# One down-projection step ahead of the third unit's state products, the fourth unit's C scaled ahead of the last w_out issue, and the fourth unit's score and state products inside the third block

## The chip, the cores and the metric

The kernel runs on one core of a Trainium2 chip. The metric is the device time of one launch in microseconds (us); a time of a version is the median of several runs.

## The reference

Two layers follow each other. The first is a chunked state-space scan over 4 batches, 8 heads and 768 positions, with 32 values and 16 state entries a head; `L` is made from the running sums of `log a`. The second is a feed-forward layer with a squared ReLU on 3072 rows of 256 values, 2048 wide inside.

```python
CB = np.einsum('bhin,bhjn->bhij', Cc, Bc)
M = CB * L                                    # L: causal decay inside a chunk
y_intra = np.einsum('bhij,bhjd->bhid', M, xc)
y_inter = np.einsum('bhin,bhnd->bhid', Cc, state) * decay_to_i[:, :, :, None]
...
state = decay_full[:, :, None, None] * state + np.sum(Bx, axis=2)
...
x = attn_out.transpose(0, 2, 1, 3).reshape(B * S, H * D)
h = np.maximum(x @ w_in, 0.0)
return (h * h) @ w_out
```

## The kernel before

The work is cut into 12 **units**, numbered from 0: one batch and 256 of its 768 positions. A unit passes through these steps, whose two-letter tokens are used in the text.

- Loads of C, B and x (`ldC`, `ldB`, `ldx`, or `ld` for all three) are issued on SyncE's queue (SP). The eight weight pieces (`wi0` to `wi3` of w_in, `wo0` to `wo3` of w_out) are issued by GpSimd (POOL). `wo3` fills the tile `w_out_b3`, which the down-projection steps 6 and 7 of every block read.
- `pc` scales C and `pb` copies B, both into the tile `jt`; `px` scales x into `xs`. `pc` and `px` stand on POOL around the change; `pb3` stands on ScalarE (ACT).
- `tr` turns `jt` over: by transposes on TensorE (PE) for units 0 to 3, by a DMA on SP from unit 4 on. `tc` copies the result from PSUM to `bct`, on VectorE (DVE) for units 2 and 3.
- `mt` makes the scores in PSUM banks 0 to 3. They leave the banks by a mask on DVE (`mk`, line 252), or by a copy on ACT (`sc`, line 257) and a later mask from that copy (`ms`, line 261).
- `u` makes the unit's state products in columns 256 to 320 of two banks (line 268, out of `xs` and `jt`), `sf` turns the first of them into a scaled state `Sd` on DVE (line 396), `in` adds the masked scores times `xs`, `ca` adds the carried state. `t` copies the sum to the tile `T`, and `us` copies the state products to the tile `us` on ACT (line 349, or line 352 where the two banks aren't neighbours).

A unit's `T` then goes through the feed-forward layer as a **block** (block a is unit 0, b is unit 1, c is unit 2), in eight steps of 256 of the 2048 columns. `c5` is four matmuls with w_in into one bank (`c5@4` names bank 4) and a ReLU on ACT that writes `hb` and frees the bank; `qc5` squares `hb` into `h` on DVE; `C5` is four matmuls with w_out that add into the block's bank 6 or 7. There are four `hb` buffers. All of these matmuls have line 459, the ReLU line 482, the square line 488.

The order of all work is written out by hand, in the string `ORDER`. Each engine takes its own instructions in that order, so an instruction that waits holds up what stands behind it on its engine. A bank may be written again only when all that reads it is done: `c1@0` must wait until bank 0 has been read out. From unit 4 on one token, `rgN`, does the bulk of a unit.

Of the kernel before, what the change touches and what calls it, by code (L numbers as in the profile page):

```python
# [30 lines left out]
def kernel(  # L31
# [20 lines left out]
        pb1:a id2:512 tr1 id3:512 tc1:1:a tc1:0:v to wo0 ms0:p sf0 sk1 px1:p jz2:p wi2 mt1 ina0 inb0 ca0 pp1:a mk1 mk1 t0:aa  # L52
        us0 sc1 mk1 fr p2@4 u1:57:6 pd us1 a0@0 a1@1 ldC2:s ina1 ms1:v wo1 wi3 pc2 inb1 sf1 ca1 qa0 t1:vv a2@2
        ldB2:s qa1 a3@3 wo2 b0@4 qa2 qa3 qb0 b1@0 qb1 b2@1 b3@5 A0 A1 B0 pb2:p tr2@23 B1 zb0 qb3 gB3:v ldx2:s ldB3:s ldC3:s ldx3:s b4@0 a4@1
        iv:32:64 zb1 tc2:1:v tc2:0:v b5@4 sb1 sb0 qb4 a5@5 qb2 qa4 mt2 sc2 B3 iv:16:32 px2 wo3 pc3 px3 mk2 mk2 sc2 A3
        A2 ms2:v ms2:v qa5 a6@4 b6@5 pb3:a B2 a7@2 qb5 b7@3 u2:45 ina2 inb2 sf2 ld4 A4 tr3@01 ca2 tc3:1:v t2:aa B4 us2 B5
        tc3:0:v qa6 u3:45 pc4 mt3 A5 us3 sc3 c5@4 qb7 qb6 mk3 za3 pb4 ldC5:s ldB5:s c3@5 qa7 c4@0 qc5 c0@1 qc3 px4 tr4 ldx5:s pb5
        pc5 sa3 c1@4 c6@5 ldC6:s tr5 ldB6:s ldx6:s qc4 qc0 A6 px5 pq A7 wm c2@0 B6 c7@1 C0 ms3:v mk3 qc6 mk3 qc7 afC2 pc6 B7
        C3 C6 C4 qc1 bk rg4 C1 qc2 d1 d0 za4 sa4 pb6 mk4 mk4 d3 mk4 C5 d4 qd0 d2 mk4 px6 tr6 ld7 C2 C7 qd1 qd2 qd3 zb3
        rg5 sb3 D0 mk5 za5 sa5 D1 mk5 d5 qd4 D2 pc7 pb7 d6 qd5 d7 qd6 D3 zb2 e0 qd7 mk5 e1 qe0 sb2 D4 mk5 D5 tr7 ld8  # L60
        e2 qe1 D6 e3 qe2 ml px7 rg6 e4 D7 qe3 za6 sa6 zb6 mk6 e5 qe4 sb6 e6 qe5 e7 qe6 iv:64:96 mk6 E0 E1 E2 E3 ldC9:s
# [836 lines left out]
```

## Time and profile before

| | |
|---|---|
| median of 3 runs | 113.89 us (113.69 to 114.79) |
| the profiled execution | 114.1 us, of which the span from first to last instruction is 112.4 us |
| busy share of the span | PE 95%, weight loads 82%, DVE 75%, ACT 68%, POOL 44% |
| granted TensorE clock | 1.00 |
| moved by DMA | 13.44 MB, mean 120 GB/s |

Rows of the trace show the start in us from the first instruction, the duration in us, the engine, the line and the operation with output and input; `x16` is a count of merged instructions, and the last bracket gives the engine's idle time ahead of them and what ended it. PEld is the weight-load half of PE, SPq and POOLq are the queues that issue DMAs. Matmuls are pipelined, so that the durations of neighbours overlap: the distance from one start to the next is what a matmul costs.

### The profile page before, as it was taken

Reading aid. Unit: us, or ns where it says so; the run is one execution under the profiler, and the core shown is the slowest. Engines: PE = TensorE matmul, PEld = TensorE weight load, DVE = VectorE, ACT = ScalarE, POOL = GpSimd, SP = SyncE. Lnnn points to the kernel's source line nnn. Section 1 sums busy time; section 2 is a strip of 40 time slices with the busy share of each in tenths; the row PEclk is TensorE's granted clock in tenths of the full one; section 3 lists DMA queues with packets and bytes.
Section 4 is the critical chain, followed back from the end, with each engine's and each line's share of the span. In section 5 each row is a group of like instructions: output and inputs, shape, how many; then the busy total and the mean of one; then the engine's idle time right before and its main releaser. Section 6 shows DMA issues by size and latency. Waiting matters only on the chain.

```text
span 112.4 us, 3682 instructions
## 1 busy us (share of the span) xinstructions
PE 107.0 (95%) x1452; PEld 91.8 (82%) x1452; DVE 84.0 (75%) x191; ACT 76.1 (68%) x156; POOL 49.9 (44%) x97
## 2 busy tenths in 40 slices
PE   6898999989999999999999999999999999999990
PEld 2335799867998989989989989889899899899980
DVE  1679997927996899969997989779489298355440
ACT  1735893884894775685687686777876867867840
POOL 7589855068286737089038644364370020000000
PEclk9999999999999999999999999999999999999999
DMA  1999999969889699999993995899582030020203
GB/s 37 199 185 140 194 193 201 183 125 168 157 151 159 72 226 135 98 186 94 99 179 39 132 235 54 100 203 95 77 205 75 0 102 0 29 70 0 93 0 93
DMA packets 67281, 13.44 MB, mean 120 GB/s; under 512 B 63104, under 2 KB 65984, under 8 KB 67264
## 3 DMA queue, kind: packets, MB, share of 16 engines
q1 hardware_dynamic: 64320, 10.88, 60.3%
q0 software_dynamic: 1664, 2.10, 11.8%
q10 hardware_dynamic: 1280, 0.23, 1.1%
q8 instruction: 11, 0.18, 0.7%
q14 instruction: 6, 0.05, 0.1%
HBM read 10.58 MB, written 3.15 MB: 122 GB/s over the span
## 4 chain that ended last, share of the span: by engine, by line
PE 74%; DMA 15%; SPq 2%; POOL 2%; DVE 1%; issue 1%; ACT 0%; DVEq 0%; ACTq 0%; POOLq 0%
PE pp L459 66%; DMA x_nat<-in_x_dram 15%; PE pp L268 5%; PE pp L237 2%; SPq L138 1%; DVE mts L252 1%; PE pp L243 1%; POOL xs L195 1%; SPq L664 1%; POOL jt L175 1%; SPq L121 0%; PE pp L213 0%; DVE xs L195 0%; ACT osl L856 0%; DVEq L626 0%
## 5 line engine op out<-in xcount | busy, mean ns | idle before, releaser
L482 ACT ACTIVATE hb<-pp 128x512 bf16<-128x512 f32 x96 | 54.4, 600 | 22.2 <-PE pp L459 21.0
L459 PE MATMUL pp<-w_out_b,h 128*128 128x256 bf16 (+1 forms) x400 | 54.0, 268 | 0.0
L459 PE MATMUL pp<-T,w_in_b 128*128 128x256 bf16 x384 | 53.4, 273 | 0.0
L488 DVE TENSOR_TENSOR h<-hb 128x512 bf16<-128x512 bf16 x96 | 45.4, 492 | 10.7 <-ACT hb L482 10.0
L459 PEld LDWEIGHTS <-w_in_b 128*128 128x128 bf16 x384 | 41.5, 114 | 1.9 <-issue 1.1
L459 PEld LDWEIGHTS <-h 128*128 128x128 bf16 x400 | 37.6, 98 | 4.5 <-issue 1.0
L252 DVE TENSOR_TENSOR mts<-pp,mask 128x512 bf16<-128x512 f32 x43 | 28.5, 678 | 0.4 <-PE pp L237 0.2
L195 POOL TENSOR_TENSOR xs<-x_nat,Pinv 128x256 bf16<-128x256 f32 (+1 forms) x19 | 13.5, 729 | 16.4 <-DMA x_nat<-in_x_dram 8.6
L384 POOL TENSOR_TENSOR Sd<-z,Pquad 128x256 bf16<-128x256 f32 x16 | 11.0, 698 | 7.8 <-DVE z L368 6.0
L175 POOL TENSOR_TENSOR jt<-C_nat,P_sb 128x128 bf16<-128x128 f32 x22 | 10.0, 476 | 9.2 <-DMA C_nat<-in_C_dram 9.2
L368 DVE SCALAR_TENSOR_TENSOR z<-z,Ptot,us 128x64 f32<-128x64 f32 x8 | 3.1, 384 | 7.0 <-ACT us L352 5.1
L562 PE MATMUL pp<-const-bfloat16-1.0 128*128 128x512 bf16 (+2 forms) x18 | 6.2, 464 | 0.8 <-PEq L882 0.8
L510 ACT COPY osb<-pp 128x512 f32<-128x512 f32 x11 | 6.4, 583 | 0.4 <-PE pp L459 0.4
L183 POOL CAST jt<-B_nat 128x256 bf16<-128x256 f32 x9 | 3.7, 412 | 5.5 <-DMA B_nat<-in_B_dram 3.9
L268 PE MATMUL pp<-mts,xs 64*32 64x128 bf16 (+1 forms) x288 | 5.3, 219 | 0.0
L268 PE MATMUL pp<-bct,Sd 128*128 128x128 bf16 x40 | 4.2, 220 | 0.0
L268 PEld LDWEIGHTS <-xs 64*32 64x32 bf16 (+1 forms) x288 | 3.4, 93 | 0.6 <-issue 0.4
L268 PEld LDWEIGHTS <-jt 64*32 64x32 bf16 (+1 forms) x128 | 1.7, 90 | 2.4 <-issue 1.1
L562 PEld LDWEIGHTS <-const-bfloat16-1.0 128*128 128x128 bf16 x18 | 1.6, 112 | 2.4 <-issue 2.2
L268 PE MATMUL pp<-xs,jt 64*32 64x64 bf16 (+1 forms) x128 | 2.9, 196 | 0.6 <-POOL xs L195 0.5
L213 PEld LDWEIGHTS <-jt 128*128 128x128 bf16 x24 | 1.5, 97 | 2.3 <-ACT jt L183 1.0
L257 ACT CAST sc<-pp 128x512 bf16<-128x512 f32 x5 | 2.9, 609 | 0.7 <-PE pp L243 0.7
(78 smaller groups left out, 59.7 us busy)
## 6 DMA issues: line engine op xcount, KB each, us to landing
out_dram<-osb SPq DMA_DIRECT2D x11, 256.0 KB, 3.0
x_nat<-in_x_dram SPq DMA_DIRECT2D x6, 256.0 KB, 5.1
w_in_b<-in_moe_w_in_dram POOLq DMA_DIRECT2D x4, 256.0 KB, 6.1
w_out_b<-in_moe_w_out_dram POOLq DMA_DIRECT2D x4, 256.0 KB, 6.3
B_nat<-in_B_dram SPq DMA_DIRECT2D x6, 128.0 KB, 5.5
C_nat<-in_C_dram SPq DMA_DIRECT2D x12, 64.0 KB, 3.8
B_nat<-in_B_dram SPq DMA_DIRECT2D x12, 64.0 KB, 3.5
x_nat<-in_x_dram SPq DMA_DIRECT2D x6, 128.0 KB, 3.4
```

Of the source, the lines that this page charges most:

```text
L175: eng.tensor_tensor(out=_fap(jt[k % 3], 128 + 144 * g, [[384, 2], [32, 4], [1, 16]]), in0=_fap(loaded[k]["C"], 128 * g, [[16, 2], [32, 4], ...
L183: fn(out=_fap(jt[k % 3], 0, [[384, 2], [16, 2], [32, 4], [1, 16]]), in_=_fap(loaded[k]["B"], 0, [[16, 2], [128, 2], [32, 4], [1, 16]]))
L195: eng.tensor_tensor(out=_fap(xs, 256 * r, [[256, 2 // n], [32, 8], [1, 32]]), in0=_fap(loaded[k]["x"], 32 * r, [[32, 2 // n], [64, 8], [1, ...
L252: nc.vector.tensor_tensor(out=live[k]["mts"][:, q].rearrange("p r g i -> p (r g i)"), in0=pp[:, q, :], in1=mask1 if k >= LATE else mask, o ...
L268: nc.tensor.matmul(dst, w, v, start=bool(need), stop=False, skip_group_check=True, **({} if pos is None else {"tile_position": pos}))
L368: nc.vector.scalar_tensor_tensor(out=z, in0=prev[0], scalar=Ptot[:, total(1, b, j - 1):total(1, b, j - 1) + 1], in1=us, op0=ALU.mult, op1= ...
L384: nc.gpsimd.tensor_tensor(out=_fap(S_d, 0, [[128, 2], [32, 4], [1, 32]]), in0=_fap(z, 0, [[32, 2], [0, 4], [1, 32]]), in1=_fap(Pquad, 4 * ...
L459: nc.tensor.matmul(dst, w(0, 128), v, skip_group_check=True, **flags)
L482: nc.scalar.activation(out=hb.rearrange("p i t -> p (i t)"), in_=pp[:, h, :], func=AF.Relu)
L488: nc.vector.tensor_tensor(out=h2, in0=hb, in1=hb, op=ALU.mult)
L510: nc.scalar.copy(out=osb, in_=pp[:, 6 if blk == 1 else 7, :])
L562: nc.tensor.matmul(pp[:, h, 0:int(cols)], ones_b[:, 0:128], ones_b[:, 0:int(cols)] if dep is None else dep, start=True, stop=True, skip_gr ...
```

## The change

Four lines of `ORDER` change; no function does.

```diff
-        ... mt2 sc2 B3 iv:16:32 px2 wo3 pc3 px3 mk2 mk2 sc2 A3
-        A2 ms2:v ms2:v qa5 a6@4 b6@5 pb3:a B2 a7@2 qb5 b7@3 u2:45 ina2 inb2 sf2 ld4 A4 tr3@01 ca2 tc3:1:v t2:aa B4 us2 B5
-        tc3:0:v qa6 u3:45 pc4 mt3 A5 us3 sc3 c5@4 qb7 qb6 mk3 za3 pb4 ldC5:s ldB5:s c3@5 qa7 c4@0 qc5 c0@1 qc3 px4 tr4 ldx5:s pb5
-        pc5 sa3 c1@4 c6@5 ldC6:s tr5 ldB6:s ldx6:s qc4 qc0 A6 px5 pq A7 wm c2@0 B6 c7@1 C0 ms3:v mk3 qc6 mk3 qc7 afC2 pc6 B7
+        ... mt2 sc2 B3 iv:16:32 px2 pc3 wo3 px3 mk2 mk2 sc2 A3
+        A2 ms2:v ms2:v qa5 a6@4 b6@5 B2 a7@2 qb5 b7@3 pb3:a qa6 A4 u2:45:2 sf2 ina2 inb2 ld4 B4 ca2 t2:va B5 tr3@01 us2
+        A5 tc3:1:v tc3:0:v c5@4 qb6 pc4 c3@5 qb7 mt3 sc3 qa7 mk3 pb4 ldC5:s ldB5:s c4@4 qc5 c0@5 qc3 u3:01 us3 za3 px4 tr4 ldx5:s pb5
+        pc5 sa3 c1@0 c6@1 ldC6:s tr5 ldB6:s ldx6:s qc4 qc0 A6 px5 pq A7 wm c2@4 B6 c7@5 C0 ms3:v mk3 qc6 mk3 qc7 afC2 pc6 B7
```

A4, the fifth down-projection step of block a, goes ahead of the state products of unit 2 (`u2`), whose first half is written to bank 2 of its own (`u2:45:2`) and scaled (`sf2`) ahead of `in` on DVE. One half of T2 is copied by DVE instead of ACT, and `us2` becomes two copies. The transposes of unit 3 (`tr3`) move behind `ca2` and B5. The scores of unit 3 (`mt3`) move behind c5 and c3, and its state products (`u3`) behind c0, in banks 0 and 1 instead of 4 and 5; the block-c steps trade banks to match. On ACT the B copy of unit 3 (`pb3`) moves behind two ReLUs.

On **POOL**, in the stretch from the x of unit 2 (`xs2`) to the x of unit 3 (`xs3`), `jt0` is the target of `pc3` and `w_out_b3` that of `wo3`. Before:

```order
L195 TENSOR_TENSOR xs2_567<-x_nat2_497,Pinv_106 128x512 [waits DMAHW6_49,DVE_49]
L160 DMA w_out_b3_119<-in_moe_w_out_dram 128x1024
L175 TENSOR_TENSOR jt0_109<-C_nat3_500,P_sb_105 128x2x4x16 [waits DMAHW0_49,PE_49]
L175 TENSOR_TENSOR jt0_109<-C_nat3_500,P_sb_105 128x2x4x16 [waits PE_49]
L195 TENSOR_TENSOR xs3_572<-x_nat3_502,Pinv_106 128x512 [waits DMAHW1_49,PE_49]
```

Now:

```order
L195 TENSOR_TENSOR xs2_567<-x_nat2_497,Pinv_106 128x512 [waits DMAHW6_49,DVE_49]
L175 TENSOR_TENSOR jt0_109<-C_nat3_500,P_sb_105 128x2x4x16 [waits DMAHW0_49,PE_49]
L175 TENSOR_TENSOR jt0_109<-C_nat3_500,P_sb_105 128x2x4x16 [waits PE_49]
L160 DMA w_out_b3_119<-in_moe_w_out_dram 128x1024
L195 TENSOR_TENSOR xs3_572<-x_nat3_502,Pinv_106 128x512 [waits DMAHW1_49,PE_49]
```

The issue of the last w_out piece stands behind the two scalings of C, which wait for a DMA. The queue of SP keeps its order.

On **ACT**, from the last ReLU of block a and b to the ReLU of c1 (`hb2_1` is the output of c1's ReLU, `sc3_0` the score copy of unit 3). Before:

```order
L183 CAST jt0_109<-B_nat3_495 128x2x2x4x16
L482 ACTIVATE hb0_7_611<-pp_120 128x512
L482 ACTIVATE hb1_7_619<-pp_120 128x512
L226 CAST T2_691<-pp_120 128x4x64 x2
L349 COPY us2_698<-pp_120 128x128
L349 COPY us3_746<-pp_120 128x128
L257 CAST sc3_0_748<-pp_120 128x512
L482 ACTIVATE hb2_5_754<-pp_120 128x512
L482 ACTIVATE hb2_3_770<-pp_120 128x512
L482 ACTIVATE hb2_4_778<-pp_120 128x512
L482 ACTIVATE hb2_0_786<-pp_120 128x512
L482 ACTIVATE hb2_1_806<-pp_120 128x512
```

Now:

```order
L482 ACTIVATE hb0_7_610<-pp_120 128x512
L482 ACTIVATE hb1_7_618<-pp_120 128x512
L183 CAST jt0_109<-B_nat3_495 128x2x2x4x16
L226 CAST T2_689<-pp_120 128x4x64
L352 COPY us2_703<-pp_120 128x64 x2
L482 ACTIVATE hb2_5_716<-pp_120 128x512
L482 ACTIVATE hb2_3_726<-pp_120 128x512
L257 CAST sc3_0_747<-pp_120 128x512
L482 ACTIVATE hb2_4_761<-pp_120 128x512
L482 ACTIVATE hb2_0_769<-pp_120 128x512
L349 COPY us3_789<-pp_120 128x128
L482 ACTIVATE hb2_1_807<-pp_120 128x512
```

The copy of unit 3's state products (`us3`) stood ahead of all of block c's ReLUs and now stands behind four of them and the score copy.

On **PE**, from c0 (the first of its matmuls) past `u3` to A6, in the changed kernel, with the waits; `T2` is block c's input and `h20_6` is A6's:

```order
L459 MATMUL pp_120<-T2_689,w_in_b0_112 128x256 [waits Activation_49]
...
L268 LDWEIGHTS jt0_109 [waits Activation_49]
L268 MATMUL pp_120<-xs3_572,jt0_109 32x64 [waits Pool_49]
...
L268 MATMUL pp_120<-xs3_572,jt0_109 32x64 [waits DVE_49]
...
L459 MATMUL pp_120<-T2_689,w_in_b0_112 128x256 [waits Activation_49]
...
L459 MATMUL pp_120<-w_out_b3_119,h20_6_621 128x256 [waits DMASW7_49]
```

Behind c0 stand the three waits of `u3` (on the score copy that clears bank 0, on `xs3`, and on the direct mask that clears bank 1), then that of c1 on `us3`, which reads bank 0, and that of A6 on the landing of `w_out_b3`. Before, `u3` stood ahead of all of block c and c1 used bank 4.

More of the change, by code (lines that the diff above doesn't have):

```diff
@@ L54 @@
         ldB2:s qa1 a3@3 wo2 b0@4 qa2 qa3 qb0 b1@0 qb1 b2@1 b3@5 A0 A1 B0 pb2:p tr2@23 B1 zb0 qb3 gB3:v ldx2:s ldB3:s ldC3:s ldx3:s b4@0 a4@1
-        iv:32:64 zb1 tc2:1:v tc2:0:v b5@4 sb1 sb0 qb4 a5@5 qb2 qa4 mt2 sc2 B3 iv:16:32 px2 wo3 pc3 px3 mk2 mk2 sc2 A3
-        A2 ms2:v ms2:v qa5 a6@4 b6@5 pb3:a B2 a7@2 qb5 b7@3 u2:45 ina2 inb2 sf2 ld4 A4 tr3@01 ca2 tc3:1:v t2:aa B4 us2 B5
-        tc3:0:v qa6 u3:45 pc4 mt3 A5 us3 sc3 c5@4 qb7 qb6 mk3 za3 pb4 ldC5:s ldB5:s c3@5 qa7 c4@0 qc5 c0@1 qc3 px4 tr4 ldx5:s pb5
-        pc5 sa3 c1@4 c6@5 ldC6:s tr5 ldB6:s ldx6:s qc4 qc0 A6 px5 pq A7 wm c2@0 B6 c7@1 C0 ms3:v mk3 qc6 mk3 qc7 afC2 pc6 B7
+        iv:32:64 zb1 tc2:1:v tc2:0:v b5@4 sb1 sb0 qb4 a5@5 qb2 qa4 mt2 sc2 B3 iv:16:32 px2 pc3 wo3 px3 mk2 mk2 sc2 A3
+        A2 ms2:v ms2:v qa5 a6@4 b6@5 B2 a7@2 qb5 b7@3 pb3:a qa6 A4 u2:45:2 sf2 ina2 inb2 ld4 B4 ca2 t2:va B5 tr3@01 us2
+        A5 tc3:1:v tc3:0:v c5@4 qb6 pc4 c3@5 qb7 mt3 sc3 qa7 mk3 pb4 ldC5:s ldB5:s c4@4 qc5 c0@5 qc3 u3:01 us3 za3 px4 tr4 ldx5:s pb5
+        pc5 sa3 c1@0 c6@1 ldC6:s tr5 ldB6:s ldx6:s qc4 qc0 A6 px5 pq A7 wm c2@4 B6 c7@5 C0 ms3:v mk3 qc6 mk3 qc7 afC2 pc6 B7
         C3 C6 C4 qc1 bk rg4 C1 qc2 d1 d0 za4 sa4 pb6 mk4 mk4 d3 mk4 C5 d4 qd0 d2 mk4 px6 tr6 ld7 C2 C7 qd1 qd2 qd3 zb3
```

## The prediction

> **What bounds the kernel now.** I first read TensorE's busy time by stretch, then its rows, then the rows of whatever released it. By stretch (core 0's busy time, granted clock, DMA share, GB/s):
>
> ```profile
> core 0: us, PE busy (x), PEclk, DMA share, GB/s
> 24.00:24.60 0.60, 0.09 (x17) 1.00 0.73 166
> 24.60:27.30 2.70, 2.65 (x78) 1.00 1.14 183
> 28.00:31.00 3.00, 3.00 (x30) 1.00 0.83 156
> 31.00:35.00 4.00, 4.00 (x39) 1.00 0.99 172
> 35.00:109.40 74.40, 74.40 (x982) 1.00 0.65 100
> ```
>
> From 28.0 to 109.4 us TensorE has no gap, at full clock. So whatever its work at 31 us gains or loses reaches the end, whole: nothing behind it has slack to give back. All that can be won here lies in the hole at 24.0 to 24.6 and in small stops up to 27.3. These are TensorE's rows there, and two of its weight loads:
>
> ```profile
> 22.98 1.04 PE L459 MATMUL pp<-T,w_in_b 128*128 128x256 bf16 x8
> 24.53 0.26 PE L268 MATMUL pp<-xs,jt 64*32 64x64 bf16 x16 [0.51 <-POOL xs L195]
> 25.10 0.61 PE L459 MATMUL pp<-w_out_b,h 128*128 128x256 bf16 x4
> 25.55 0.72 PE L213 MATMUL pp<-eye_b,jt 128*128 128x128 bf16 x6
> 25.86 0.23 PEld L213 LDWEIGHTS <-jt 128*128 128x128 bf16 x4 [0.22 <-POOL jt L175]
> 26.10 0.28 PE L268 MATMUL pp<-bct,Sd 128*128 128x128 bf16 x2
> 26.21 1.04 PE L459 MATMUL pp<-w_out_b,h 128*128 128x256 bf16 x8
> 27.18 0.21 PEld L268 LDWEIGHTS <-jt 64*32 64x32 bf16 x13 [0.21 <-ACT us L349]
> 27.26 0.26 PE L268 MATMUL pp<-xs,jt 64*32 64x64 bf16 x16
> 27.44 0.42 PE L243 MATMUL pp<-bct 32*64 32x256 bf16 x16
> 27.80 0.61 PE L459 MATMUL pp<-w_out_b,h 128*128 128x256 bf16 x4
> 28.24 2.78 PE L459 MATMUL pp<-T,w_in_b 128*128 128x256 bf16 x24
> 30.86 1.04 PE L459 MATMUL pp<-w_out_b,h 128*128 128x256 bf16 x8
> ```
>
> In order: a7 and b7, `u2` (waits for `xs2`), A4, `tr3` (waits for `pc3`), `ca2`, B4 and B5, `u3` (waits for `us2`), `mt3`, A5, the six steps c5, c3, c4, c0, c1, c6, and A6 with A7. A step of four matmuls costs (30.86 - 28.24) / 6 = 0.44 us.
>
> **The gain, worked out.** Three stops go. The step ahead of `u2` fills the hole: `u2` starts at 24.53 in both, since the x of unit 2 decides it, and A4 (0.44 us) is done before it, at 24.3 by slots. The stop at `tr3` (0.22, from `pc3`) goes, since `pc3` is earlier and `tr3` later. The stop at `u3` (0.17 of start to start, 27.09 to 27.26) goes from there. Together 0.83 us. The transposes, `u3` and `mt3` keep their counts.
>
> Its slots after, by the same row distances: `u2` 24.53, B4 25.10, `ca2` 25.55, B5 25.66, `tr3` 26.10 (six at 0.06, as four took from 25.86 to 26.10), A5 26.43, c5 26.87, c3 27.31, `mt3` 27.74, c4 28.10. If nothing else waited, A6 would start at 30.86 - 0.83 = 30.03. Two things are late next.
>
> **First, the scalar engine's order.** These rows are of ACT and of DVE:
>
> ```profile
> 27.61 0.27 ACT L349 COPY us<-pp 128x128 f32<-128x128 f32 x1 [0.66 <-PE pp L268]
> 27.91 0.59 ACT L257 CAST sc<-pp 128x512 bf16<-128x512 f32 x1
> 28.93 3.05 ACT L482 ACTIVATE hb<-pp 128x512 bf16<-128x512 f32 x6 [0.43 <-PE pp L459]
> 26.30 0.62 DVE L228 COPY bct<-pp 128x384 bf16<-128x384 bf16 x2 [0.63 <-PE pp L213]
> 26.84 1.73 DVE L488 TENSOR_TENSOR h<-hb 128x512 bf16<-128x512 bf16 x3
> 28.49 0.68 DVE L252 TENSOR_TENSOR mts<-pp,mask 128x512 bf16<-128x512 f32 x1
> ```
>
> A ReLU starts 28.93 - 28.24 = 0.69 after its step; the six follow each other every 0.48 and the last takes 0.64. Before, `us3` and `sc3` ran while TensorE was at A5, and the ReLUs had 0.43 idle ahead of them. After, in ACT's order: c5's ReLU 27.56, c3's 28.04, `sc3` 28.52 to 29.11, c4's ReLU 29.0, c0's 29.48, `us3` 29.96 to 30.23. With 0.05 from a release to TensorE (24.48 to 24.53 at `xs2`), c4 starts at 28.2, c0 at 28.69, and `u3` at 29.16. Its second half also needs the mask of bank 1. DVE copies `bct3` 0.2 after `tr3`, from 26.63; three squares and the mask follow as above, 0.33 later than before: the mask ends at 28.49 + 0.33 + 0.68 = 29.50, `u3`'s second half starts at 29.55, and 27.61 - 27.26 = 0.35 later `us3` could start. So ACT's queue (29.96) decides by a hair, with DVE at 29.90 close behind.
>
> c1 goes to bank 0, which `us3` reads: it starts at 30.28, c6 at 30.72, **A6 at 31.16**, which is 0.30 later than the 30.86 of before. TensorE stands still for some 0.6 us between `u3` and c1, where it never stood before. If POOL's C scalings slow the squares less in their new place, only the 29.90 moves, not the 29.96.
>
> **Second, the last w_out piece.** POOL's rows, SP's issue of the third C, and landing times of DMAs:
>
> ```profile
> 23.43 1.05 POOL L195 TENSOR_TENSOR xs<-x_nat,Pinv 128x512 bf16<-128x512 f32 x1 [3.98 <-DMA x_nat<-in_x_dram]
> 24.42 0.61 POOL L160 DMA_DIRECT2D w_out_b<-in_moe_w_out_dram  x1
> 25.05 0.77 POOL L175 TENSOR_TENSOR jt<-C_nat,P_sb 128x128 bf16<-128x128 f32 x2
> 26.15 1.05 POOL L195 TENSOR_TENSOR xs<-x_nat,Pinv 128x512 bf16<-128x512 f32 x1 [0.34 <-DMA x_nat<-in_x_dram]
> 18.07 1.90 SPq L138 DMA_DIRECT2D C_nat<-in_C_dram  x1
> C_nat<-in_C_dram SPq DMA_DIRECT2D x1, 128.0 KB, 6.4
> w_out_b<-in_moe_w_out_dram POOLq DMA_DIRECT2D x1, 256.0 KB, 5.9
> DMA to landing us min/median/max: 5.9/6.3/7.1
> DMA to landing us min/median/max: 5.6/6.1/8.3
> ```
>
> (The last two rows are of all four w_out and all four w_in pieces; the row above them is that of `wo3`.) Before, the piece landed at 24.42 + 5.9 = 30.3, and A6 wanted it at 30.86: 0.5 us to spare. After, `pc3` comes first, and C of unit 3 lands only at 18.07 + 6.4 = 24.5; with 0.1 to start and 0.77 of work POOL issues `wo3` at 25.3. Landing is a new unknown. From below, a load of the same 256 KB on SP a little later took 3.6 us:
>
> ```profile
> x_nat<-in_x_dram SPq DMA_DIRECT2D x1, 256.0 KB, 3.6
> ```
>
> That would be 28.9 and free. From above, 8.3 gives 33.6, 2.8 us late. I take its own 5.9: the DMA share in its flight is no lower after the shift (1.14, 0.83, 0.99 above). So it lands at 31.2, and **A6 starts at 31.26**.
>
> The Trainium skill ("DMA: Bandwidth & Descriptors", section "Anatomy of one DMA — SWDGE (gpsimd) path") fits such a load as 2.0 us plus bytes over 436 KB per us, an estimate of 2.6 us here. By that the piece would be there long before A6, and the sum would rest on `us3` alone, +0.3. This trace disagrees, with 5.6 at the least in eight loads among other traffic.
>
> **The sum.** The two waits lie over each other, so the later counts: 31.26 - 30.86 = +0.4. The 0.83 won is spent by 31 us, and 0.4 more. The other edits cost nothing:
>
> ```profile
> L228 DVE CAST T<-pp 128x256 bf16<-128x256 f32 x2 | 0.7, 416 | 0.0
> L352 ACT COPY us<-pp 128x64 f32<-128x64 f32 x6 | 1.3, 243 | 0.0
> ```
>
> The `T2` half on DVE (0.42 us) and the two `us2` copies (0.24 each) fall beside B5, `tr3` and A5 with c5 not due until 26.87; if that cover went, each would cost at most its own length. `pb3` behind two ReLUs ends near 25.1, a microsecond ahead of `tr3`; SP's issues keep their order; `px3` waits for its x until 26.15 either way, as the issue of `wo3` ends at 25.9. Behind A6, qc0 and bank 4 and 5 are ready a microsecond before C0 and c2 want them.
>
> Against the profiled execution that is 114.1 + 0.4 = 114.5; the median of before lies 0.2 lower, so I forecast 113.89 + 0.4 = **114.3 us** for the median.
>
> **The rivals.**
>
> *The gain is kept.* If the piece lands in time and ACT and DVE are quick enough that c4, c0 and `u3` keep their slots, `u3` starts at 28.98; `us3` still follows it by 0.35 and takes 0.27, so c1 starts at 29.65 and A6 at 30.53, which is -0.33: 113.6. The full 0.83 can't stay, since c1 needs `u3`'s own copy. For it speaks that the hole at 24.0 is surely filled. Against it, ACT must do four ReLUs and a score copy between 27.56 and `us3`, five at 0.48, which is 2.4 us. Chance 0.10.
>
> *No net change*, from 0.2 below to 0.2 above: ACT or DMA a little quicker than summed, gain and waits even. 0.16.
>
> *Slower, by late weights.* It is the landing of `w_out_b3` alone, at A6. It decides from a landing after 31.1, and beyond +0.8 from 6.3 us of flight on. A flight of 7.1, the worst of the four, gives A6 at 32.45, +1.6: 115.5. For it: two of the four w_out pieces took over 6.3, and the piece now shares its flight with x of unit 4 and C and B of unit 5 for longer. Against it: those slow ones were issued among three other weight pieces, and this one is alone on its queue. Chance 0.14, about half of it past +1.1.
>
> *The change doesn't do what it says*: A4 could itself be late and push `u2`.
>
> ```profile
> 16.30 0.61 POOL L160 DMA_DIRECT2D w_out_b<-in_moe_w_out_dram  x1
> 22.50 0.76 DVE L488 TENSOR_TENSOR h<-hb 128x512 bf16<-128x512 bf16 x2
> ```
>
> Its weights (the first row) are there by 16.30 + 7.1 = 23.4 even with the slowest flight; its square stands ahead of those of a5 and b5 (the second row), which end at 23.3. Its slot is 23.85, and it would have to lose 0.24 us to move `u2`. It is inside the other cases.
>
> **How the numbers follow.** The forecast (+0.2 to +0.8) has 0.60, the rivals 0.10, 0.16 and 0.14. The likeliest is 114.3. About 1%, 1.1 us, is what a measurement of this kernel tells from no change. Faster than that needs more than the whole 0.83, 0.02. Slower needs a flight over 6.6 us, 0.08. Within is 0.90. The range reaches from -0.4 (the gain as far as it can be kept) to +1.4 (a flight of 6.9): 113.5 to 115.3.
>
> **What would show it.** In the profile after: TensorE's first row behind a7 and b7 has line 459 and starts near 23.85, and `u2` stays near 24.5; `tr3` and `u3` have no stop from POOL's `jt` or from `us2`; a new idle time of some 0.6 us stands between `u3` and c1, ended by the copy `us` of line 349; the w_out issue stands at 25.3, with 5.9 to landing; A6 starts near 31.3. Wrong would be: c1 without a wait, a landing before 30.5, or any new gap in TensorE behind 32 us.

## The result, and the profile after

The changed kernel takes 114.92 us (median of 20 runs, 114.41 to 118.63) against 114.16 us for the kernel before, run beside it. By the ratio it is 1.0085 times the time of before, 95% interval 1.0061 to 1.011. That is some 0.97 us slower. A second measurement (after_again) gave 1.0112 (1.0074 to 1.015), some 1.3 us. Ratios are what is compared throughout: a few executions of either kernel are disturbed and longer, the medians hold them and the ratios don't, and the profiles of e3_again and e9_before_pad are of such executions. The profiled execution took 114.87 us with a span of 113.2 us (before: 114.1 and 112.4).

TensorE by stretch, as before (core 0's busy time, granted clock, DMA share, GB/s):

```profile
core 0: us, PE busy (x), PEclk, DMA share, GB/s
24.00:24.60 0.60, 0.58 (x6) 1.00 1.08 247
28.00:31.00 3.00, 1.90 (x44) 1.00 0.97 161
31.00:35.00 4.00, 4.00 (x39) 1.00 0.89 152
35.00:110.00 75.00, 75.00 (x989) 1.00 0.60 99
```

The hole at 24.0 to 24.6 is filled, as forecast. The stretch from 28 to 31, which had no gap, now has 1.1 us of them. Behind it nothing changed. TensorE's rows show where the 1.1 us lie:

```profile
23.11 1.04 PE L459 MATMUL pp<-T,w_in_b 128*128 128x256 bf16 x8
23.98 0.60 PE L459 MATMUL pp<-w_out_b,h 128*128 128x256 bf16 x4
24.68 0.25 PE L268 MATMUL pp<-xs,jt 64*32 64x64 bf16 x16
27.01 1.04 PE L459 MATMUL pp<-T,w_in_b 128*128 128x256 bf16 x8
27.98 0.42 PE L243 MATMUL pp<-bct 32*64 32x256 bf16 x16
28.65 1.08 PE L459 MATMUL pp<-T,w_in_b 128*128 128x256 bf16 x8 [0.25 <-ACT hb L482]
29.67 0.25 PE L268 MATMUL pp<-xs,jt 64*32 64x64 bf16 x16
30.77 1.03 PE L459 MATMUL pp<-T,w_in_b 128*128 128x256 bf16 x8 [0.85 <-ACT us L349]
31.64 1.04 PE L459 MATMUL pp<-w_out_b,h 128*128 128x256 bf16 x8
```

These are a7 and b7; A4; `u2`; c5 and c3; `mt3`; c4 and c0, which wait for a ReLU; `u3`; c1 and c6, which wait for the copy `us3`; A6 and A7. The copy that c1 waits for is the one the prediction named. ACT's rows lead up to it:

```profile
26.27 0.34 ACT L352 COPY us<-pp 128x64 f32<-128x64 f32 x2
28.00 1.09 ACT L482 ACTIVATE hb<-pp 128x512 bf16<-128x512 f32 x2 [1.39 <-issue]
28.97 0.59 ACT L257 CAST sc<-pp 128x512 bf16<-128x512 f32 x1
29.44 1.12 ACT L482 ACTIVATE hb<-pp 128x512 bf16<-128x512 f32 x2
30.40 0.31 ACT L349 COPY us<-pp 128x128 f32<-128x128 f32 x1
```

From c5's ReLU (28.00) ACT runs without a pause through c3's ReLU, `sc3`, and the ReLUs of c4 and c0 to `us3`, 2.40 us later. That ReLU itself starts 28.00 - 27.01 = 0.99 us behind its step, where before it took 0.69. The 0.30 between is put down to "issue": ACT waited for nothing that the profile shows. The w_out issue (POOL, between `xs2` and `xs3`, and the piece's time to landing) stands where it was expected:

```profile
23.30 1.33 POOL L195 TENSOR_TENSOR xs<-x_nat,Pinv 128x512 bf16<-128x512 f32 x1 [3.92 <-DMA x_nat<-in_x_dram]
25.29 0.60 POOL L160 DMA_DIRECT2D w_out_b<-in_moe_w_out_dram  x1
25.98 1.04 POOL L195 TENSOR_TENSOR xs<-x_nat,Pinv 128x512 bf16<-128x512 f32 x1
w_out_b<-in_moe_w_out_dram POOLq DMA_DIRECT2D x1, 256.0 KB, 5.5
```

It lands at 25.29 + 5.5 = 30.8, and A6 starts at 31.64. So the piece is 0.8 us early and A6 waits only for its turn behind c6.

The open question was why the loss is twice the forecast. Two theories stood at the start. By the first, c1's wait for `us3` is the whole loss and the gain ahead of it is real. By the second, the late weights hold A6. (A third, that `u3` waits for a later `xs3`, falls already here: `xs3`, POOL's last row above, ends at 25.98 + 1.04 = 27.02, and `u3` starts at 29.67.) The runs brought another: the holes of before are slack in part, and filling them is worth little.

### The profile page after: what moved, and what is told of

The parts are those of the page before. It is cut to its first block, busy times and chain, and to the rows that moved or that the text cites. A ratio compares the mean times of both kernels' runs of the same rounds, so it can differ in the third digit from the quotient of the medians.

```text
span 113.2 us, 3683 instructions
## 1 busy us (share of the span) xinstructions
PE 107.5 (95%) x1452; PEld 91.9 (81%) x1452; DVE 83.4 (74%) x192; ACT 75.6 (67%) x156; POOL 50.6 (45%) x97
## 4 chain that ended last, share of the span: by engine, by line
PE 72%; DMA 15%; DVE 3%; SPq 2%; issue 2%; POOL 1%; ACT 1%; DVEq 0%; ACTq 0%; POOLq 0%
PE pp L459 64%; DMA x_nat<-in_x_dram 15%; PE pp L268 6%; PE pp L237 2%; DVE mts L252 1%; SPq L138 1%; POOL xs L195 1%; DVE h L488 1%; SPq L664 1%; PE pp L243 1%; DVE bct L228 1%; ACT hb L482 0%; DVE xs L195 0%; SPq L121 0%; PE pp L213 0%
## 5 line engine op out<-in xcount | busy, mean ns | idle before, releaser
L488 DVE TENSOR_TENSOR h<-hb 128x512 bf16<-128x512 bf16 x96 | 44.3, 478 | 12.4 <-ACT hb L482 11.6
L195 POOL TENSOR_TENSOR xs<-x_nat,Pinv 128x256 bf16<-128x256 f32 (+1 forms) x19 | 14.0, 749 | 16.0 <-DMA x_nat<-in_x_dram 7.5
L183 POOL CAST jt<-B_nat 128x256 bf16<-128x256 f32 x9 | 4.3, 480 | 5.6 <-DMA B_nat<-in_B_dram 4.4
L268 PEld LDWEIGHTS <-Sd 128*128 128x128 bf16 x40 | 3.1, 98 | 0.4
L156 POOL DMA_DIRECT2D w_in_b<-in_moe_w_in_dram x4 | 3.1, 774 | 0.1
```

The lines of the kernel that those rows point to most:

```text
L183: fn(out=_fap(jt[k % 3], 0, [[384, 2], [16, 2], [32, 4], [1, 16]]), in_=_fap(loaded[k]["B"], 0, [[16, 2], [128, 2], [32, 4], [1, 16]]))
L195: eng.tensor_tensor(out=_fap(xs, 256 * r, [[256, 2 // n], [32, 8], [1, 32]]), in0=_fap(loaded[k]["x"], 32 * r, [[32, 2 // n], [64, 8], [1, ...
L268: nc.tensor.matmul(dst, w, v, start=bool(need), stop=False, skip_group_check=True, **({} if pos is None else {"tile_position": pos}))
L488: nc.vector.tensor_tensor(out=h2, in0=hb, in1=hb, op=ALU.mult)
```

## The experiments

All twelve runs follow, with the two profiles that were shown. "a7 to A6" is the time from the start of a7 to that of A6 in the run's trace; it is the stretch that the change rewrites. From the start of A6 TensorE needs 78.35 us to the start of its last matmul in every one of these traces but that of e5_bank0. So a trace's time is set by where A6 stands, and A6 by two things, where a7 stands and the stretch between them.

| run | a7 | A6 | a7 to A6 | ratio to before (95%) |
|---|---|---|---|---|
| before (the profile shown) | 22.98 | 30.86 | 7.88 | 1 |
| before_again | 23.95 | 30.96 | 7.01 | 1.0008 (0.997 to 1.0046) |
| after (the profile shown) | 23.11 | 31.64 | 8.53 | 1.0085 (1.0061 to 1.011) |
| after_again | 23.50 | 32.04 | 8.53 | 1.0112 (1.0074 to 1.015) |
| e1_banks | 23.87 | 31.66 | 7.79 | 1.0065 (1.0025 to 1.0106) |
| e2_wo3_first | 23.57 | 32.11 | 8.53 | 1.018 (1.0108 to 1.0252) |
| e3_a4_alone | 23.84 | 31.15 | 7.31 | 1.0033 (0.9996 to 1.007) |
| e3_again | 25.36 | 32.68 | 7.32 | 0.9987 (0.9952 to 1.0022) |
| e4_u3_early | 23.84 | 31.22 | 7.38 | 1.0032 (0.9996 to 1.0068) |
| e5_bank0 | 23.57 | 30.79 | 7.22 | 1.0013 (0.9977 to 1.0049) |
| e6_pad_act | 23.25 | 31.32 | 8.07 | 1.0068 (1.0028 to 1.0108) |
| e7_swap_alone | 23.74 | 30.75 | 7.01 | 1.0011 (0.9977 to 1.0045) |
| e8_banks_pad | 23.16 | 30.81 | 7.65 | 0.999 (0.9952 to 1.0028) |
| e9_before_pad | 25.39 | 32.40 | 7.01 | 1.0019 (0.9969 to 1.0069) |

**e1_banks: c1 no longer waits for `us3`.** The changed kernel with block c's banks traded back at one place.

```diff
-        pc5 sa3 c1@0 c6@1 ... wm c2@4 B6 c7@5 C0
+        pc5 sa3 c1@4 c6@5 ... wm c2@0 B6 c7@1 C0
```

> The changed kernel with one edit: c1 and c6 take banks 4 and 5, c2 and c7 take 0 and 1, as in the kernel before. Theory A (c1 waits for the copy of unit 3's state products, because it goes to bank 0, which that copy reads at the end of the scalar engine's queue): c1 now waits only for c4's ReLU to clear bank 4, which ended at 30.07 in the profile after, so c1 starts near 30.12 instead of 30.77 and A6 near 31.05 instead of 31.64: 0.6 us less than the changed kernel, about 0.2 more than the kernel before. Theory B (the last w_out piece is late): no change against the changed kernel, since its issue is untouched. Theory C (the third unit's state products start later because their scaled x is later): no change either.

TensorE's rows of this run:

```profile
23.87 1.04 PE L459 MATMUL pp<-T,w_in_b 128*128 128x256 bf16 x8
29.27 1.09 PE L459 MATMUL pp<-T,w_in_b 128*128 128x256 bf16 x8 [0.26 <-ACT hb L482]
30.28 0.25 PE L268 MATMUL pp<-xs,jt 64*32 64x64 bf16 x16
30.73 1.09 PE L459 MATMUL pp<-T,w_in_b 128*128 128x256 bf16 x8 [0.20 <-ACT hb L482]
31.66 1.04 PE L459 MATMUL pp<-w_out_b,h 128*128 128x256 bf16 x8
```

The wait of 0.85 is gone from c1, and 0.20 for bank 4's own ReLU has come instead. a7 to A6 shrinks by 0.74. Of that 0.65 is c1's; another 0.18 lies between A4 and `u2` (0.70 in the first profile of after, 0.52 here), which this edit doesn't touch, and some 0.09 is given back at other places. The time stays at 1.0065, with an interval that overlaps that of the change, and A6 stands where it stood in the first profile of after, because a7 itself came 0.76 later in this execution. So c1's wait is confirmed as a term of the stretch, and something else is at work in the time.

**e2_wo3_first: the weights land early.** The changed kernel with the w_out issue back ahead of the C scaling.

```diff
-        ... px2 pc3 wo3 px3
+        ... px2 wo3 pc3 px3
```

> The changed kernel with one edit: the issue of the last w_out piece stands ahead of the scalings of the fourth C again, as in the kernel before. Theory A (bank 0): no change against the changed kernel within 0.1 us, since the piece landed at 30.8, 0.9 us before A6 wanted it; it should land near 30.2 now. Theory B (late weights, or their traffic): faster than the changed kernel by 0.3 us or more.

```profile
24.03 0.61 POOL L160 DMA_DIRECT2D w_out_b<-in_moe_w_out_dram  x1
w_out_b<-in_moe_w_out_dram POOLq DMA_DIRECT2D x1, 256.0 KB, 5.1
31.24 1.03 PE L459 MATMUL pp<-T,w_in_b 128*128 128x256 bf16 x8 [0.85 <-ACT us L349]
```

The piece lands at 24.03 + 5.1 = 29.1 and nothing gets faster: c1 waits the same 0.85, a7 to A6 is the same 8.53, and the ratio is no lower than that of the change (its interval is wide, from six runs). The late weights are not the cause.

**e3_a4_alone: the filled hole alone.** The kernel before with A4 ahead of `u2` and nothing else.

```diff
-        ... qb5 b7@3 u2:45 ina2 inb2 sf2 ld4 A4 tr3@01
+        ... qb5 b7@3 A4 u2:45 ina2 inb2 sf2 ld4 tr3@01
```

> The kernel before with one edit: A4 stands ahead of the third unit's state products, nothing else moves. If the hole ahead of them is TensorE time that can be won (the step of the prediction that counted 0.83 us): 0.4 us faster than the kernel before. If the stops behind it are set by other engines (the scaled state of unit 2 on DVE, the scaled C of unit 3 on POOL until 25.8, the scaled x of unit 3 on POOL until 27.2): the time that A4 gives up ahead of the transposes becomes a wait there, unit 3's state products start at 27.26 as before, and the time is that of the kernel before within 0.1 us.

It gains nothing: 1.0033, and 0.9987 when it was measured once more.

> The kernel before with A4 alone moved ahead of unit 2's state products, a second time. From a7 to A6 it took 7.31 us, 0.57 less than the kernel before, though its time wasn't lower. If the stop at A0 hid the gain, then with like stops in both it is 0.3 to 0.5% faster than the kernel before run beside it; if moving A4 gains nothing, the stretch from a7 to A6 is 7.8 or more here.

The two intervals share 0.9996 to 1.0022. The stretch didn't behave as the second expectation had it: it set 7.8 us or more for "moving A4 gains nothing", and the trace has 7.32 with no gain in the time that can be told. Part of the explanation is in the first trace's weight loads, where a new stop has come behind A4's old place:

```profile
26.45 0.11 PEld L268 LDWEIGHTS <-Sd 128*128 128x128 bf16 x2 [0.30 <-DVE Sd L396]
```

`ca2` now waits for the scaled state, and the 7.31 us are 0.30 more than the 7.01 of the next run. The larger part shows in the repeat of the unchanged kernel.

**before_again and after_again: both kernels unchanged**, profiled once more.

> The kernel before, unchanged, for a second profile beside the others. In the experiments so far TensorE reached a7 at 23.6 to 23.9 us, against 23.0 and 23.1 in the first two profiles, by a stop of 0.2 to 0.8 us always behind the second weight load of A0, where the code is the same in all. If that stop is an accident of the run, it may show here too, and a7 to A6 stays at 7.9 us; if it belongs to the edited kernels, a7 is at 23.0 here. Time: that of the kernel before.

> The changed kernel, unchanged, for a second profile. From a7 to A6 it took 8.53 us in the first profile, 0.65 more than the kernel before. Theory A (bank 0 holds c1 back until the copy of unit 3's state products): again near 8.5, with a wait of 0.8 us ahead of c1, and about 0.6% slower than the kernel before. If the longer time comes from what lies ahead of a7, the stretch differs by less than 0.3 between the two.

TensorE's rows of before_again: a0 and a1, which wait for a w_in piece, `tr2`, which waits for the copy of B on POOL, a7 and b7, `u2`, `u3`, A6:

```profile
12.38 1.06 PE L459 MATMUL pp<-T,w_in_b 128*128 128x256 bf16 x8 [0.58 <-DMA w_in_b<-in_moe_w_in_dram]
18.34 0.51 PE L213 MATMUL pp<-eye_b,jt 128*128 128x128 bf16 x6 [0.30 <-POOL jt L183]
23.95 1.04 PE L459 MATMUL pp<-T,w_in_b 128*128 128x256 bf16 x8
24.91 0.25 PE L268 MATMUL pp<-xs,jt 64*32 64x64 bf16 x16
27.35 0.25 PE L268 MATMUL pp<-xs,jt 64*32 64x64 bf16 x16
30.96 1.04 PE L459 MATMUL pp<-w_out_b,h 128*128 128x256 bf16 x8
```

Here a7 comes 0.97 later than in the first profile, most of it by the two waits shown. The hole ahead of `u2` isn't there, nor the stop at `u3`, and still A6 stands at 30.96 against 30.86, and the span is the same 112.4. TensorE is busy for all of the 7.01 us. So in the kernel before, the stops between a7 and `u3` are slack which takes up as much as 7.88 - 7.01 = 0.87 us of what the work ahead of a7 loses. When a7 is early, TensorE waits for POOL: for `xs2`, for `pc3` at `tr3`, and for `xs3`, which ends at 26.15 + 1.05 = 27.20 in the first profile and lets `u3` start at 27.26. (The prediction put that last stop down to `us2`, which ended at 26.95.) When a7 is late, TensorE doesn't wait. POOL was earlier too in before_again (`xs2` at 21.82, not 23.43), but its times of the first profile, 24.48, 25.82 and 27.20, wouldn't have held anything up here either. A6 comes out at about 30.9 in both. It need not always: the executions of the kernel before that this ratio rests on take from 113.23 to 114.91 us.

The rows of after_again, the step A0, a7 and b7, and A6:

```profile
16.80 1.26 PE L459 MATMUL pp<-w_out_b,h 128*128 128x256 bf16 x10 [0.57 <-issue]
23.50 1.04 PE L459 MATMUL pp<-T,w_in_b 128*128 128x256 bf16 x8
32.04 0.71 PE L459 MATMUL pp<-w_out_b,h 128*128 128x256 bf16 x5
```

A stop inside A0 delays a7 by 0.39 against the first profile of after, and A6 comes 0.40 later. The changed kernel passed this delay on to the end, and e2_wo3_first did the same with 0.46 us, since its own stops (8.53 - 7.01 = 1.52 us, the same in three traces) hang for the most part on TensorE's own progress: all but some 0.2 of them begin with c5's ReLU and shift with it. Against traces without them they are 0.31 ahead of c4, 0.92 between `u3` and c1, and 0.17 ahead of `u2`; small ones make up the rest. That the last is alike in the three is chance: in the first profile of after `u2` waits for `xs2`, in the other two for the ReLU of a7 to leave bank 2, into which the change moved it.

**e4_u3_early and e5_bank0: `u3` back ahead of block c.** e4_u3_early is the changed kernel with the w_out issue first, `u3` ahead of c5 and in other banks; e5_bank0 also puts the first half of `u2` into bank 0.

```diff
-        ... px2 pc3 wo3 px3 ... B5 tr3@01 us2
+        ... px2 wo3 pc3 px3 ... B5 tr3@13 us2
-        A5 tc3:1:v tc3:0:v c5@4 ... qc3 u3:01 us3 za3 px4
+        A5 tc3:1:v tc3:0:v u3:02 us3 za3 c5@4 ... qc3 px4
```

> The changed kernel with the state products of unit 3 and their copy directly behind A5, in banks 0 and 2 (the transposes of unit 3 in banks 1 and 3), ahead of all of block c, and with the last w_out issue ahead of the fourth C's scaling. Theory A: the copy is first in the scalar engine's queue instead of last, c1 waits for bank 0 only until the score copy has left it, near 29.5, A6 starts near 30.4 (before 30.86): 0.4 us faster than the kernel before, 1.2 faster than the changed kernel. If the hole's gain can't be kept for another reason, the time is that of the kernel before or worse.

> As the experiment with the state products of unit 3 directly behind A5, but unit 2's first state products go to bank 0 instead of bank 2, which a7's ReLU had to clear first (unit 2's products waited for it, 25.15 to 25.40). Expected: from a7 to A6 7.1 us (7.38 with bank 2, 7.88 in the kernel before), and 0.5 to 0.7% faster than the kernel before if the front is alike in both.

TensorE's rows of e4_u3_early, c4, c0, c1 and c6 without a stop, then A6:

```profile
29.38 2.00 PE L459 MATMUL pp<-T,w_in_b 128*128 128x256 bf16 x16
31.22 1.04 PE L459 MATMUL pp<-w_out_b,h 128*128 128x256 bf16 x8
```

With `us3` ahead of block c's ReLUs, a7 to A6 falls to 7.38 and 7.22 (the 0.16 between them is the wait for bank 2, gone from e5_bank0), and the time is that of before (1.0032 and 1.0013). So the loss hangs on the late `u3`. Both still have A4 ahead of `u2`, and the gain of 0.4 us or more that was expected of each didn't come: it would be a ratio of 0.9965, below both intervals. In e5_bank0's profile A6 stands at 30.79, but a wait for a DMA near 65 us took 0.6 back; that was seen in one execution only and was not followed.

**e6_pad_act: the stop of ACT.** The changed kernel with six tiny copies in ACT's program near its start, where ACT is idle.

```diff
-        ... sp la1:a pbh0:p hd
+        ... sp la1:a wa pbh0:p hd
+                "wa": lambda: [A.copy(out=warm, in_=ones_b[:, 0:2]) for _ in range(6)],
```

> The changed kernel with six tiny copies (128x2) put into ACT's program near its start, where ACT is idle. They move every later ACT instruction by six places in the program and change nothing else. In the changed kernel c5's ReLU starts 1.40 us after the end of the us2 copies, with an idle time put down to issue, 0.3 us after its matmuls would have allowed. Theory that this stop hangs on the place in ACT's program (a fetch of instructions): the stop goes or moves elsewhere, c5's ReLU follows its step by 0.7 us, c1 starts some 0.3 us earlier against a7 and a7 to A6 takes 8.2 instead of 8.53 us; the time is 0.2 to 0.3 below that of the changed kernel, so 0.6 to 0.8 us over before. Rival, that c5's ReLU waits for something of the order itself (bank, buffer, T2): still 1.40 us after us2, a7 to A6 8.5, 0.9 to 1.3 us over before.

Rows of TensorE and ACT:

```profile
27.00 1.04 PE L459 MATMUL pp<-T,w_in_b 128*128 128x256 bf16 x8
28.33 1.09 PE L459 MATMUL pp<-T,w_in_b 128*128 128x256 bf16 x8
30.45 1.03 PE L459 MATMUL pp<-T,w_in_b 128*128 128x256 bf16 x8 [0.84 <-ACT us L349]
26.26 0.34 ACT L352 COPY us<-pp 128x64 f32<-128x64 f32 x2
27.68 1.09 ACT L482 ACTIVATE hb<-pp 128x512 bf16<-128x512 f32 x2 [1.09 <-issue]
```

c5's ReLU now starts 27.68 - 27.00 = 0.68 behind its step, the 0.69 of before. c4 no longer waits, and c1 starts 0.32 earlier while c5 stands at the same time. a7 to A6 is 8.07, 0.46 less, of which 0.31 is the stop and 0.17 lies ahead of `u2`, which doesn't wait in this execution. The stop therefore hangs on the place of the instructions in ACT's program and not on the order of the work. The time, 1.0068, can't be told from that of the change. Whether the stop is a fetch of instructions stays open: the trace's small transfers on the queues marked "instruction" keep no fixed distance to it (the last 8 KB piece to land ahead of the ReLU does so 0.50 us before it in after and 0.03 in after_again, with the same 0.30 of stop).

**e7_swap_alone: the C scaling first, in the kernel before.**

```diff
-        ... px2 wo3 pc3 px3
+        ... px2 pc3 wo3 px3
```

> The kernel before with one part of the change alone: C of unit 3 is scaled ahead of the issue of the last w_out piece. The piece should be issued at 25.3 us and, with the flight of 5.5 us seen in the changed kernel, land at 30.8, where A6 stands at 30.9. Theory that the piece never binds: the same time as before within 0.2 us, A6 at 30.9. Rival that the late piece was part of the loss (my prediction's deciding wait): A6 starts only behind a landing after 31.0 and the time is 0.3 to 0.5 us over before. The stop at tr3 should shrink, since C of unit 3 is scaled 0.6 us earlier; by the slack theory that gives no gain at the end, by the prediction's sum of stops it would give 0.2 us.

```profile
17.04 1.27 PE L459 MATMUL pp<-w_out_b,h 128*128 128x256 bf16 x10 [0.81 <-issue]
23.74 1.04 PE L459 MATMUL pp<-T,w_in_b 128*128 128x256 bf16 x8
30.75 1.04 PE L459 MATMUL pp<-w_out_b,h 128*128 128x256 bf16 x8
25.28 0.60 POOL L160 DMA_DIRECT2D w_out_b<-in_moe_w_out_dram  x1
w_out_b<-in_moe_w_out_dram POOLq DMA_DIRECT2D x1, 256.0 KB, 5.1
```

No difference (1.0011), and the landing at 25.28 + 5.1 = 30.4 is in time. This execution shows the slack best: TensorE stood still for 0.81 us in A0, more than in any other trace here, and A6 is nevertheless at 30.75.

**e8_banks_pad: both waits gone.** The changed kernel with the edits of e1_banks and e6_pad_act together.

> The changed kernel with both of its new waits taken away: c1 and c6 in banks 4 and 5 as before the change (as in e1_banks), and the six tiny ACT copies near the start (as in e6_pad_act). If the wait of c1 on the copy us3 and the stop of ACT ahead of c5's ReLU are the whole loss, they add up: a7 to A6 takes 7.8 - 0.4 = 7.3 to 7.4 us (7.0 is the bare work), A6 starts near 31.0, and the time is that of before within 0.3 us. Rival, that something else of the change costs the rest (A4 ahead of u2, the later transposes, the w_out piece): a7 to A6 stays near 7.8 or A6 waits elsewhere, and the time stays 0.6 us or more over before.

Rows of TensorE (a7 and b7; c4 and c0; `u3`; c1 and c6; A6) and the w_out issue:

```profile
23.16 1.04 PE L459 MATMUL pp<-T,w_in_b 128*128 128x256 bf16 x8
28.24 1.09 PE L459 MATMUL pp<-T,w_in_b 128*128 128x256 bf16 x8
29.25 0.25 PE L268 MATMUL pp<-xs,jt 64*32 64x64 bf16 x16
29.71 1.09 PE L459 MATMUL pp<-T,w_in_b 128*128 128x256 bf16 x8 [0.20 <-ACT hb L482]
30.81 1.03 PE L459 MATMUL pp<-w_out_b,h 128*128 128x256 bf16 x8
24.63 0.60 POOL L160 DMA_DIRECT2D w_out_b<-in_moe_w_out_dram  x1
w_out_b<-in_moe_w_out_dram POOLq DMA_DIRECT2D x1, 256.0 KB, 6.1
```

The time is that of before, 0.999. Each of the two edits alone left the kernel at 1.0065 and 1.0068; together the loss is gone. a7 to A6 is 7.65 and not the expected 7.3 to 7.4. The reason stands in the last rows: A6 starts 1.10 behind c1, where two steps take 0.87, and the piece lands at 24.63 + 6.1 = 30.7. So here, with c1 out of the way, the weights do hold A6, by 0.2 us. They were the next wait, hidden behind c1's.

**e9_before_pad: the padding alone**, the same six copies in the kernel before.

> The kernel before with the six tiny ACT copies alone: what the padding itself does. Expected: nothing within 0.2 us, A6 at 30.8 to 31.0, since ACT is idle where they stand and its later work there has 0.4 us of idle time ahead of c5's ReLU. Rival: the place in ACT's program matters in before as well (a stop elsewhere comes or goes), so that the time moves by 0.3 us or more, and the gain of e6_pad_act against the changed kernel is no property of the change.

1.0019, with an interval of half a per cent to both sides: no difference that can be told. It excludes a gain from the padding beyond 0.0031, which is 0.35 us, too wide to say more. Its profile has a7 at 25.39, so that A6 can't be held against the 30.8 to 31.0 that were expected, but the stretch is the bare 7.01.

No version here beats the kernel before.

## Why the prediction was right or wrong

**The direction and the mechanism held.** A4 runs in the hole, the new idle time lies between `u3` and c1 and is ended by `us3`, TensorE has no new gap behind 32 us, and the time is in the range. The size did not: 0.97 us (1.3 in the second measurement) against a forecast of 0.4, past the +0.2 to +0.8 that the prediction gave most of its chance to. Above +0.8 its range was there for a late weight piece, so that the time lies inside it is in part luck. Step by step:

- *A4 in the hole, slots to c5.* Right within this profile. From a7 to c5 the prediction has 26.87 - 22.98 = 3.89 us; measured are 27.01 - 23.11 = 3.90.
- *The scalar engine's order, c1 at 30.28.* The right wait, mis-sized: **a stop of ACT was counted at nothing.** From c5's ReLU to `us3` the slots say 29.96 - 27.56 = 2.40 and the trace says 2.40. But c5's ReLU came at 28.00: 0.14 because c5 itself was later, and 0.30 for a stop of ACT that no row of before shows. c1 came at 30.77, 0.49 late. By `us3` alone the prediction had A6 at 31.16, +0.3; with the 0.49 it is the 31.64 of the profile, +0.78.
- *"The gain, worked out", 0.83.* **This step failed as well,** though not in this pair of profiles, where the slots show that the stops were filled. They were there in the one execution shown, but they don't belong to every execution. Where a7 comes at 23.95 or 23.74 they don't exist, and A6 stands at 30.96 and 30.75 all the same. e3_a4_alone, e4_u3_early and e5_bank0 fill the hole and win nothing. The prediction took 22.98 as fixed and set the new waits against stops that are gone in other executions. There the change gives up no stop and adds 1.52 us of its own: from before_again to after_again A6 moves by 1.08. This fits that the ratios lie 0.2 and 0.5 us above the +0.78, but the interval of the first reaches down to 0.70 us, so this share of the miss is argued and not measured.
- *The last w_out piece, which was to decide.* Wrong as the deciding wait: 5.5 in flight, not 5.9, and a landing 0.8 us ahead of A6. It was to decide by 0.1 us (31.26 against 31.16), where the flight of this load differs by 1.7 us among the traces. The swap alone (e7_swap_alone) and its undoing (e2_wo3_first) both change nothing. That A6 would be held by it if c1 were not was right, as e8_banks_pad shows. By the rule that the prediction cited from the Trainium skill ("DMA: Bandwidth & Descriptors", "Anatomy of one DMA — SWDGE (gpsimd) path") the sum would have rested on `us3` alone. That came true, though not for its reason: flights of 4.4 to 6.1 us in these traces stand against the 2.6 us estimated from that page.
- *The rivals.* "The gain is kept" and "No net change" fall with the ratio's interval. "Slower, by late weights" has the right sign and the wrong cause. "The change doesn't do what it says" falls, since A4 didn't push `u2` in this profile: `u2` follows `xs2`, which ends at 23.30 + 1.33 = 24.63.

What stays open: what the stop of ACT is, and how often a7 is early or late. The traces do show what makes it late, the waits of before_again for a w_in piece and for POOL's copy of B, and in others the stop inside A0; why these differ from one execution to the next they don't show.

## What to carry to other kernels

Before you count an idle stretch as a gain, profile the kernel before a second time: if the work ahead of it comes later and the stretch shrinks by as much with the same end, it is slack set by another chain, and in such executions filling it wins nothing. A reordering that moves a wait from "until a transfer is there" to "until my own earlier result has come back" can cost more than its length, since it no longer takes up delays from ahead. Where two waits end close together, taking one away shows the next, so a repair has to be tried with all of them gone.

## What the runs showed of the hardware that was not expected

TensorE can stop inside A0, always behind its second matmul, put down to "issue": by 0.22 to 0.81 us in seven of the fourteen traces (0.57 and 0.81 in the rows above), by some 0.1 in three more, and not in the two profiles of the kernel before. It comes and goes with executions of different kernels, so it isn't a matter of the change. The traces point to its cause. A 16 KB transfer on a queue that the profile marks "instruction" lands at 15.2 to 15.7 us in these seven and at 14.7 to 15.1 in the other seven. The third matmul of A0 never starts less than 1.3 us behind that landing, and in the seven with the stop it starts 1.3 to 1.5 behind it. That TensorE waits there for its instructions is thus argued from fourteen traces; no run moved the transfer by itself.

ACT stood still for 0.30 us ahead of c5's ReLU in the changed kernel, at the same distance behind the `us2` copies in each of its traces that keep the order up to there (after, after_again, e1_banks, e2_wo3_first), and six tiny copies put in 20 us earlier removed it (0.99 to 0.68 us from step to ReLU). This stop was removed by padding; whether others come and go with edits that shift an engine's program was not tried.

The same 256 KB load, issued on POOL between 22.8 and 25.9 us, took 4.4 to 6.1 us in the fourteen traces. That spread of 1.7 us is what a margin for such a load has to cover here.
